# A fused adaLN attention block: the loads, the zero products and the first query evacuation of the prologue rearranged

## Chip, cores and metric

The kernel runs on one core of one Trainium2 chip. The metric is the device time of one launch in microseconds (us); a kernel is timed in several runs and the median counts. The profile is of one execution, whose span (first to last instruction of the core) is a little shorter than its device time.

## What is computed

The reference, cut to what matters (batch 1, 2048 tokens, width 512, 32 heads of 16, hidden width 1376):

```python
mod = (silu(c) @ w_mod).reshape(1, 6, 1, 512)       # sa, ca, ga, sb, cb, gb
h = layernorm(x) * (1 + ca) + sa
q, k, v = heads(h @ wqkv)
o = softmax(q @ k.T * 16 ** -0.5) @ v               # 32 heads, 2048 x 2048 scores each
x = x + ga * (o @ wo)
h = layernorm(x) * (1 + cb) + sb
x = x + gb * (gelu(h @ w1 + b1) @ w2 + b2)
```

## The kernel before, in words

Tokens lie in four blocks of 512 (`xb[0]` to `xb[3]`), channels in four chunks of 128. Four heads share a 128-row chunk in two parities, so a "quad" is (query block, chunk, parity): four heads, one in each 32-row strip of TensorE. One unit of work is one strip of one quad against one tile of 128 keys: a product of 32 rows into a PSUM bank (line 905), then the exponential, then the product with V (line 1144). The exponential is shared out: ScalarE takes two or three banks in one ACTIVATE (line 1382, tiles `PB` and, early, `TB`), VectorE takes others by writing a 16-bit integer that is read as a float (line 1526) and shifting it for its second and third copies (line 1560).

The program has two parts. The **prologue** (lines 141 to 393) is written out by hand: loads are issued, 12 zero products are put on TensorE (`turn_over(WARM[0])`, line 362), VectorE takes the statistics of `xb[0]` (line 212, four tiles), aggregates them (217), GpSimd makes the reciprocal root `rs` (222, 223), `silu_c` makes `sc_bf` from the condition vector `cc_bf` (an exponential on ScalarE, line 197, and three small VectorE operations, 198 to 200), TensorE makes the first shift and scale (32 products with one column, line 245, weights `W_m0`), three more zero products follow (`turn_over(WARM[1])`), VectorE normalises `xb[0]` (231), TensorE turns it (16 transposes, line 377), `hT` is evacuated by VectorE (274) and ScalarE (271) in turn, and chunk 0 of K and Q is projected (line 385, K and Q alternating over four pieces, weights `W_k` and `W_q`). `kT` is evacuated by ScalarE (285). The query has two masked halves: VectorE writes `qm[:, 0]` (388), ScalarE `qm[:, 1]` (389); the second is read only by quads of the second parity.

Loads go out on two queues, each in program order: SP's has half of `xb[0]`, half of `W_m0`, `W_k`, `W_q`, `W_v`, `xb[2]`, `xb[3]`, `W_m1`, later `W_m2` and `W_o`; ScalarE's has the other half of `xb[0]`, `cc_bf` (512 elements of two bytes, each to a place of its own), the other half of `W_m0` and `xb[1]`. Each large load is 512 KB (`W_m1`, `W_m2`: 1 MB).

The **body** is written by a planner that runs while the program is built. It keeps a clock for each engine (`clk`), assumed durations and due times, and emits one instruction after another; the order on each engine is then fixed, and the chip only waits on semaphores. `dve_load` adds up the VectorE work that is outstanding, and `d_wanted` offers further scores to VectorE only while that is below a limit, `D_LOAD` (1700 before). Where TensorE has nothing to do in the plan, `pe_idle` writes a zero product (line 1225 or 1228). `FRONT` holds the times at which the planner takes `W_v` and the blocks of `xb` for loaded. A **tail** ends the program: the last half block's output projection, second layernorm, MLP (lines 730 to 812) and stores.

Of the kernel before, what the change touches and what calls it, by code (L numbers as in the profile page):

```python
# [20 lines left out]
P = 128  # L21
# [30 lines left out]
D_BANKS = (5, 6, 2)  # L52
BG_BANKS = (2, 5, 6)
BG_STRICT = False
D_LOAD = 1700.0
X_FREE = 1
D_ALONE = 900.0
A_SLACK = 1350.0
OVER = 180.0
PART_MIN = 3  # L60
PV_FIRST = 99
D_SOON = 400.0
A_MIN = 600.0
D_WAIT = 350.0
POOL_WAIT = 4000.0
POOL_COVER = 1100.0
LOCK_WAIT = 100.0
TIE = 60.0
T_NEED = 1
T_NEXT = 1  # L70
T_OPEN = 0.0
ROOT = 1000.0
ROOT_L = 700.0
SPREAD = (0.9, 0.9, 0.65)
WARM = (12, 3)
FRONT = (1200.0, 0.0, 2600.0, 4000.0)
AHEAD = 32
T_KEEP = 3
# [22 lines left out]
def adaln_block(ctx: ExitStack, tc: tile.TileContext, A_x, A_wqkv, A_wo, B_x, B_w1, B_b1, B_w2, B_b2,  # L101
# [43 lines left out]
    for i, eng in enumerate((nc.sync, nc.scalar)):  # L145
        for t in (2 * i, 2 * i + 1):
            eng.dma_start(out=xb[0][:, t, :], in_=x_tok[0][:, t, :])
    nc.scalar.dma_start(out=cc_bf, in_=c.rearrange("o (j p) -> p (o j)", p=P))
    for i, eng in enumerate((nc.sync, nc.scalar)):
        eng.dma_start(out=W_m0[:, 2 * i:2 * i + 2, :], in_=wm_v[:, 2 * i:2 * i + 2, 0:2 * D])  # L150
    nc.sync.dma_start(out=W_k, in_=wqkv_v[:, :, D:2 * D])
    nc.scalar.dma_start(out=xb[1], in_=x_tok[1])
    nc.sync.dma_start(out=W_q, in_=wqkv_v[:, :, 0:D])
    nc.sync.dma_start(out=W_v, in_=wqkv_v[:, :, 2 * D:3 * D])
    for b in range(2, NQB):
        nc.sync.dma_start(out=xb[b], in_=x_tok[b])
    W_m1 = load_mod(1, nc.sync)


    AFTER = mybir.DependencyInfo(mybir.DependencyClass.Sync, mybir.DependencyReason.SCHED_ONLY)  # L160
# [203 lines left out]
    turn_over(WARM[0])  # L364
    st0 = pron.tile([P, 12, 6], FP32, name="st1")
    for t in range(4):
        ln_stats(xb[0], st0, t, t)
    psm = bk(7, FP32, 16)
    mv0, rs0 = ln_rstd(st0, 4)
    silu_c()  # L370
    first_mod_mm(psm)
    turn_over(WARM[1])
    turned = [bk(2 + j, BF16) for j in range(NC)]
    for t in range(4):
        ln_norm(xb[0], xb[0], mv0, rs0, t, t)
# [10 lines left out]
    k_evac(psk, 0, 0, "act")  # L386
    qm[(0, 0)] = qmp.tile([P, 2, 512], BF16, name="qm")
    nc.vector.tensor_scalar(out=qm[(0, 0)][:, 0, :], in0=psq, scalar1=qmask[:, 0:1], scalar2=None, op0=ALU.mult)
    nc.scalar.mul(out=qm[(0, 0)][:, 1, :], in_=psq, mul=qmask[:, 1:2])
    W_m2 = load_mod(2, nc.sync)  # L390
    nc.sync.dma_start(out=W_o, in_=A_wo.rearrange("(j p) n -> p j n", p=P))

# [109 lines left out]

    rdy[("k", 0, 0)], rdy[("q", 0, 0)] = 800.0, 1000.0
    rdy["wv"] = FRONT[0]
    for b in (1, 2, 3):
        rdy[("x", b)] = FRONT[b]
    for j in range(NC):
# [348 lines left out]
    def dve_cost(n):  # L856
        return 67.0 + 533.0 * n

    clk = {"PE": 0.0, "ACT": 1350.0, "DVE": 950.0, "POOL": 0.0}
    mode = [None]  # L860
    free = [0.0] * 6 + [850.0, 0.0]
    rowq = [[(qi, kt) for qi in range(QN) for kt in tiles_of(qi)] for _ in range(4)]
# [19 lines left out]
    outs = deque()  # L882
    stat = {"d": 0, "groups": 0, "part": 0, "bursts": 0}

    def item_ok(qi, kt, t):
        b, tq = quads[qi]
        ch = tq // 2
        return has([("k", ch, x // 4) for x in kt] + [("q", ch, b)], t)

    def tok_of(qi):  # L890
        if qi < LAST:
# [69 lines left out]
    def d_wanted(t):  # L961
        if len(d_fill) >= 2 or not any(rowq):
            return False
        if sum(len(q) for q in rowq) < 10:
            return False
        need = T_NEED if not units or len(units[-1]["it"]) == 2 else 0
        if need and min(q[0][0] for q in rowq if q) > cur[0]:
            need += T_NEXT
        if need and sum(1 for x in tslot if x <= t) < need + int(T_OPEN * len(units)):
            return False  # L970
        return dve_load(t) < D_LOAD

    def bg_bank(t):
        for i in ((6,) if X_BOTH else (5, 6)) if scored[0] < X_FRONT else BG_BANKS if any(rowq) else (2, 5, 6, 0, 1, 3, 4):
# [41 lines left out]
    def pe_burst(t, z):  # L1016
        bs = list(ZONES[z]) if z is not None else []
        x = EXTRA[z] if z is not None else None
        if scored[0] < X_FRONT:
            if z is not None:  # L1020
                x = 2 if z == 0 else 5 if X_BOTH else None
            if x is not None and free[x] <= t:
                bs.append(x)
        elif (x is not None and free[x] <= t and not (busy_sum[0] is None and reserve(t))
                and sum(1 for i in D_BANKS if free[i] <= t) > X_FREE):
            bs.append(x)
        take = []
        held_ = later_held()
        for r in lag_rows():
            if len(take) == len(bs):  # L1030
                break
            k = first_ok(r, t, held_ + len(take))
            if k is not None:
                take.append((r, k))
        if z is not None and len(take) < len(bs):
            more = [(r, k + 1) for r, k in take if len(rowq[r]) > k + 1 and item_ok(*rowq[r][k + 1], t)
                    and (rowq[r][k + 1][0] == rowq[r][k][0] or not k)]
            take += more[:len(bs) - len(take)]
        if z is not None and not take:
            return False  # L1040
        picked = [(r, rowq[r][k]) for r, k in take]
        for r, x in picked:
            rowq[r].remove(x)
        used = [r for r, _ in take]
        dp = []
        if d_wanted(t):
            for r in d_rows(used):
                k = next_d(r, t)
                if k is None:
                    continue  # L1050
                b_ = next((i for i in D_BANKS if free[i] <= t and i not in bs[:len(take)] + [x[0] for x in dp]), None)
                if b_ is None:
                    break
                if (not BG_STRICT and busy_sum[0] is None and reserve(t)
                        and sum(1 for i in BG_BANKS if free[i] <= t and i not in FLEX) - len(dp) < 2):
                    break
                dp.append((b_, r, rowq[r].pop(k)))
                if len(dp) + len(d_fill) >= 2 or z is not None and len(dp) + len(take) >= 4:
                    break
                u = units[-1] if units else None  # L1060
                if u is None or len(u["it"]) + len(dp) == 2:
                    break
        if z is None and not dp:
            return False
        go("q")
        t0 = clk["PE"]
        rows = [r for r, _ in picked] + [r for _, r, _ in dp]
        first = len(set(rows))
        clk["PE"] = t0 + group(first) + (group(len(rows) - first) if len(rows) > first else 0.0)
        ready = clk["PE"] + L_PE  # L1070
        qk([(b_, qi, kt, r) for (r, (qi, kt)), b_ in zip(picked, bs)] + [(b_, qi, kt, r) for b_, r, (qi, kt) in dp])
        for (r, (qi, kt)), b_ in zip(picked, bs):
            free[b_] = INF
        if z is not None:
            zone_busy[z] = True
            filled.append((z, [(qi, kt, r) for r, (qi, kt) in picked], clk["PE"] + L_PA))
        for b_, r, (qi, kt) in dp:
            free[b_] = INF
            if not units or len(units[-1]["it"]) == 2:
                s = next(i for i in range(NT) if tslot[i] <= t)  # L1080
                tslot[s] = INF
                units.append({"it": [], "a": {"s": s}, "j": 0, "n": 0})
            u = units[-1]
            u["it"].append((qi, kt, r))
            todo[qi][r] += NV - 1
            claimed[qi][r] += 1
            d_fill.append((b_, u, len(u["it"]) - 1, ready))
            stat["d"] += 1
        stat["bursts"] += 1
        return True  # L1090

    def pv_ready(t, press):
        qi = cur[0]
        if qi >= QN:
            return None
        if not od_open[0] and od_free[0] > t:
            return None
        g = []
        most = max(todo[qi])
        closed = not any(left[qi])  # L1100
        for r in range(4):
            e = entries[qi][r]
            if todo[qi][r] == 0:
                continue
            if e and e[0][0] <= t + 20 and has([("vv", x, e[0][3]) if e[0][3] else ("v", x) for x in e[0][2]], t):
                g.append(r)
            elif not (closed and todo[qi][r] < most) and not press:
                return None
        return g or None
# [132 lines left out]
    def step_pe_work(t):  # L1242
# [5 lines left out]
        tried = False  # L1248
        dw = d_wanted(t)
        d_at = min((free[i] for i in D_BANKS), default=INF)  # L1250
        later = dw and t < d_at < t + D_SOON and slack - (d_at - t) > A_MIN
        if fill_z is not None and slack < A_SLACK and not later:
            if pe_burst(t, fill_z):
                return True
            tried = True
        nxt = INF
        if any(rowq) and not tried:
            if fill_z is not None:
                nxt = max(t + max(0.0, slack - A_SLACK), d_at if later else 0.0)
            else:  # L1260
                cand = [max(free[i] for i in ZONES[z]) for z in (0, 1) if max(free[i] for i in ZONES[z]) < INF]
                if cand:
                    nxt = max(min(cand), t + slack - A_SLACK)

        if t > pe_at[0] + 700.0:
            nxt = INF

        def fits(x, m):
            return t + x + (0 if mode[0] == m else MODE) <= nxt + OVER
        if dw and dve_load(t) < D_ALONE and fits(226.0, "q") and nxt > t + D_WAIT:  # L1270
            if pe_burst(t, None):
                return True
        press = p_free() < 3 or sum(1 for x in tslot if x <= t) < 2
# [8 lines left out]
                return True  # L1282
        if not g:
            g = pv_ready(t, True)
            if g and len(g) < PART_MIN:
                g = None
        if g and fits(226.0, "p"):
            pe_pv(t, g)
# [459 lines left out]
```

## Time and profile before

| | us |
|---|---|
| median of 3 runs (757.05 to 758.9) | 757.85 |
| the profiled execution: device time | 755.97 |
| its span | 754.2 |
| TensorE busy in the span, zero products included | 736.8 |
| ScalarE busy | 721.3 |
| VectorE busy | 701.1 |
| GpSimd busy | 110.8 |
| first exponential of the body begins | 18.90 |

A row of the timeline is: start in us, duration in us, engine, line, operation, output <- input, form, count, and in brackets how long the engine sat idle before it and what ended that. Rows are merged where like instructions follow each other; SPq and ACTq are DMA issues on these queues. A row of the windows has a stretch, its length, and the busy time (and count) of each engine, then the granted TensorE clock, the DMA share and GB/s.

### The profile page before, as it was taken

The page shows a single profiled execution, that of the slowest core. Times are in us where ns is not written, and L with a number is a line of the kernel's source. Part 1 is how long each engine was busy: PE and PEld are TensorE (multiplying, and loading weights), DVE is VectorE, ACT ScalarE, POOL GpSimd, SP SyncE. Part 2 cuts the span into 40 slices and gives each one's busy share as a digit, 9 for nine tenths or more (in the row PEclk, how much of TensorE's full clock was granted, in tenths as well). Part 3 has the DMA queues.
Part 4 walks back from the last instruction along what each step waited for, and adds up shares of the span by engine and source line. Part 5 has one row for each costly group of instructions (what it writes and reads, how often), then busy time and mean ns, then how long its engine had stood idle before and what let it go on. Part 6 is the DMA issues. An engine that isn't in the chain of part 4 may idle for free. (4 is left out here: it accounts for less than half of the span.)

```text
span 754.2 us, 21382 instructions
## 1 busy us (share of the span) xinstructions
PE 736.8 (98%) x8858; PEld 257.9 (34%) x8861; DVE 701.1 (93%) x1444; ACT 721.3 (96%) x736; POOL 110.8 (15%) x136
## 2 busy tenths in 40 slices
PE   7999999999999999999999999999999999999997
PEld 3333332222333333224222232322233322444454
DVE  4976999999999999999999999999999999999983
ACT  2999999999999999999999999999999999999993
POOL 2424010311222310101001020100101110010000
PEclk8999999999999999999999999999999999999999
DMA  8200000001400100000001000000001010000000
GB/s 287 105 2 3 17 9 9 5 10 34 135 10 9 38 9 10 3 9 10 17 17 46 10 10 10 10 23 16 14 10 53 6 23 10 12 22 20 6 7 32
DMA packets 28456, 20.49 MB, mean 27 GB/s; under 512 B 14545, under 2 KB 24402, under 8 KB 28354
## 3 DMA queue, kind: packets, MB, share of 16 engines
q1 hardware_dynamic: 24914, 15.04, 7.6%
q10 hardware_dynamic: 3440, 4.03, 1.7%
q8 instruction: 71, 1.16, 0.7%
q14 instruction: 31, 0.25, 0.1%
HBM read 16.45 MB, written 2.61 MB: 25 GB/s over the span
## 5 line engine op out<-in xcount | busy, mean ns | idle before, releaser
L1382 ACT ACTIVATE PB<-PS 128x1024 bf16<-128x1024 f32 (+1 forms) x689 | 672.7, 1204 | 3.4 <-PE PS L905 2.0
L1526 DVE TENSOR_SCALAR TB<-PS 128x512 int16<-128x512 f32 (+1 forms) x527 | 367.2, 711 | 9.1 <-PE PS L905 7.6
L905 PE MATMUL PS<-qm,kT 32*128 32x512 bf16 (+1 forms) x2304 | 294.8, 358 | 3.2 <-ACT PB L1382 1.6
L1144 PE MATMUL PS<-PB,VE 128*32 128x512 bf16 (+1 forms) x1653 | 251.2, 361 | 0.0
L1560 DVE TENSOR_SCALAR TB<-TB 128x1024 int16<-128x1024 int16 x556 | 222.5, 424 | 4.6 <-PE PS L905 0.5
L1144 PE MATMUL PS<-TB,VV 128*32 128x512 f16 (+1 forms) x1246 | 217.9, 360 | 0.4 <-DVE TB L1560 0.2
L905 PEld LDWEIGHTS <-kT 32*128 32x128 bf16 x2304 | 82.7, 91 | 255.6 <-issue 251.6
L1144 PE MATMUL PS<-TB,VE 128*32 128x512 f16 (+2 forms) x651 | 148.4, 362 | 0.9 <-DVE o_sb L1475 0.5
L1144 PEld LDWEIGHTS <-VE 128*32 128x32 bf16 x2304 | 70.3, 94 | 78.3 <-issue 73.1
L1225 PE MATMUL PS<-W_q,zero 128*32 128x256 bf16 x471 | 94.0, 273 | 2.5 <-DVE TB L1526 1.8
L1144 PEld LDWEIGHTS <-VV 128*32 128x32 bf16 x1246 | 56.2, 95 | 40.2 <-issue 36.9
L1503 POOL TENSOR_TENSOR o_sb<-o_sb,rb 128x512 f32<-128x512 f32 (+1 forms) x16 | 19.3, 1204 | 253.4 <-DVE TB L1560 208.1
L1225 PEld LDWEIGHTS <-zero 128*32 128x32 bf16 x471 | 42.7, 96 | 33.1 <-issue 10.6
L1503 POOL TENSOR_TENSOR OT<-o_sb,rb 128x512 bf16<-128x512 f32 (+1 forms) x16 | 19.3, 1205 | 212.5 <-DVE TB L1560 154.3
L442 PE MATMUL PS<-h2T,W 128*32 128x512 bf16 x528 | 45.4, 383 | 0.0
L442 PE MATMUL PS<-W,uG 128*32 128x512 bf16 x528 | 45.4, 383 | 0.0
L645 DVE TENSOR_SCALAR uG<-PS,b1c 128x512 bf16<-128x512 f32 x33 | 24.6, 746 | 0.0
L442 PE MATMUL PS<-W_o,OT 128*32 128x512 bf16 x272 | 22.5, 383 | 0.0
L317 DVE CAST VE<-PS 128x512 bf16<-128x512 f32 x16 | 11.0, 687 | 11.4 <-PE PS L442 11.4
L1475 DVE COPY o_sb<-PS 128x512 f32<-128x512 f32 (+1 forms) x32 | 20.8, 649 | 0.7 <-PE PS L1144 0.7
L322 POOL TENSOR_SCALAR VV<-VE 128x512 bf16<-128x512 bf16 x12 | 18.0, 1504 | 21.5 <-DVE VE L317 21.0
L442 PE MATMUL PS<-hT,W_q 128*32 128x512 bf16 x240 | 21.0, 384 | 0.0
(122 smaller groups left out, 429.2 us busy)
## 6 DMA issues: line engine op xcount, KB each, us to landing
rb<-d SPq DMA_DIRECT2D x112, 32.0 KB
W_m<-in_w_mod_dram SPq DMA_DIRECT2D x2, 1024.0 KB
out_dram<-ob SPq DMA_DIRECT2D x16, 128.0 KB
xr<-in_A_x_dram SPq DMA_DIRECT2D x3, 512.0 KB
W<-in_B_w_dram ACTq DMA_DIRECT2D x1, 1376.0 KB
W<-in_B_w_dram ACTq DMA_DIRECT2D x1, 1280.0 KB
xb<-in_A_x_dram SPq DMA_DIRECT2D x2, 512.0 KB
W_m<-in_w_mod_dram SPq DMA_DIRECT2D x1, 512.0 KB
```

The lines of the kernel that those rows point to most:

```text
L317: nc.vector.tensor_copy(out=dst, in_=src)
L322: return nc.gpsimd.tensor_scalar(out=dst, in0=src, scalar1=WJ[j], scalar2=None, op0=ALU.mult)
L442: nc.tensor.matmul(out=ps[cols, :], lhsT=lhsT[:, cols], rhs=rhs, start=start, stop=stop)
L645: return lambda ps, e: nc.vector.tensor_scalar(out=T["u"][:, fc, :], in0=ps, scalar1=late["b1c"][:, fc:fc + 1], scalar2=None, op0=ALU.add)
L905: nc.tensor.matmul(out=bk(bank)[:, seg(qi, i)], lhsT=kT[32 * r:32 * r + 32, ch, kt[i] * P:(kt[i] + 1) * P], rhs=qm[(b, ch)][32 * r:32 * r ...
L1144: nc.tensor.matmul(out=PS[32 * r:32 * r + 32, 7, tok_of(qi)], lhsT=wt, rhs=src[:, seg(qi, i)], start=not started[qi][r], stop=todo[qi][r] ...
L1225: nc.tensor.matmul(out=PS[0:32, b_, 0:256], lhsT=zero, rhs=W_q[:, 0, 0:256], start=True, stop=True)
L1382: nc.scalar.activation(out=dst, in_=PS[:, b0:b0 + n, :], func=ACT.Exp, bias=-KEXP * math.log(2.0), scale=math.log(2.0) / STEP)
L1475: made = nc.vector.tensor_copy(out=o[:, cs], in_=PS[:, 7, cs])
L1503: return nc.gpsimd.tensor_tensor(out=(o if par else ot)[:, cs], in0=o[:, cs], in1=rb[:, cs], op=ALU.mult)
L1526: made = nc.vector.tensor_scalar(out=TB[:, u["a"]["s"], i:i + n, :], in0=PS[:, b0:b0 + n, :], scalar1=T_BIAS, scalar2=0.0, op0=ALU.add, op ...
L1560: made = nc.vector.tensor_scalar(out=TB[:, s, 0:n, :], in0=TB[:, a["s"], 0:n, :], scalar1=float(MJ[j] - MJ[j - 1]), scalar2=None, op0=ALU.add)
```

## The change

1. `cc_bf` is loaded from GpSimd's queue, ahead of everything else on it, in place of ScalarE's.
2. All loads after `xb[0]`, `cc_bf` and `W_m0` go on SP's queue, and the first of them, `W_k`, waits until the second of the four statistics of `xb[0]` is made. The order is then `W_k`, `W_q`, `xb[1]`, `W_v`, `xb[2]`, `xb[3]`, `W_m1`.
3. `WARM` goes from (12, 3) to (16, 3), and the call that used the 3 goes: 16 zero products before the first shift and scale, none between it and the transposes.
4. `qm[:, 1]` is no longer evacuated in the prologue but is a step of the planner on ScalarE, which may come behind the first exponentials; quads of the second parity wait for it (label `q01`), and the planner takes ScalarE for free at 650 in place of 1350.
5. The planner's constants become a table by stage whose rows are all alike. All values are those of before but `D_LOAD`, which goes from 1700 to 1900.

```diff
-D_LOAD = 1700.0
+TUNE = ((1900.0, 900.0, 1350.0, 180.0, 400.0, 600.0, 3, 1),) * 17
-WARM = (12, 3)
+WARM = (16, 3)
...
-    nc.scalar.dma_start(out=cc_bf, in_=c.rearrange("o (j p) -> p (o j)", p=P))
+    nc.gpsimd.dma_start(out=cc_bf, in_=c.rearrange("o (j p) -> p (o j)", p=P))
     for i, eng in enumerate((nc.sync, nc.scalar)):
         eng.dma_start(out=W_m0[:, 2 * i:2 * i + 2, :], in_=wm_v[:, 2 * i:2 * i + 2, 0:2 * D])
-    nc.sync.dma_start(out=W_k, in_=wqkv_v[:, :, D:2 * D])
-    nc.scalar.dma_start(out=xb[1], in_=x_tok[1])
-    nc.sync.dma_start(out=W_q, in_=wqkv_v[:, :, 0:D])
-    nc.sync.dma_start(out=W_v, in_=wqkv_v[:, :, 2 * D:3 * D])
-    for b in range(2, NQB):
-        nc.sync.dma_start(out=xb[b], in_=x_tok[b])
-    W_m1 = load_mod(1, nc.sync)
...
     turn_over(WARM[0])
     st0 = pron.tile([P, 12, 6], FP32, name="st1")
     for t in range(4):
-        ln_stats(xb[0], st0, t, t)
+        seen = nc.vector.bn_stats(out=st0[:, t, :], in_=xb[0][:, t, :])
+        if t == 1:
+            held = nc.sync.dma_start(out=W_k, in_=wqkv_v[:, :, D:2 * D])
+            tc.add_manual_dep(held.ins, seen.ins.name, AFTER, reason="order of loads")
+            nc.sync.dma_start(out=W_q, in_=wqkv_v[:, :, 0:D])
+            nc.sync.dma_start(out=xb[1], in_=x_tok[1])
+            nc.sync.dma_start(out=W_v, in_=wqkv_v[:, :, 2 * D:3 * D])
+            for b in range(2, NQB):
+                nc.sync.dma_start(out=xb[b], in_=x_tok[b])
+            W_m1 = load_mod(1, nc.sync)
...
-    turn_over(WARM[1])
...
-    nc.scalar.mul(out=qm[(0, 0)][:, 1, :], in_=psq, mul=qmask[:, 1:2])
...
+    op("ACT", 690.0, lambda: nc.scalar.mul(out=qm[(0, 0)][:, 1, :], in_=psq, mul=qmask[:, 1:2]), "q01", [], 5)
...
-    clk = {"PE": 0.0, "ACT": 1350.0, "DVE": 950.0, "POOL": 0.0}
+    clk = {"PE": 0.0, "ACT": 650.0, "DVE": 950.0, "POOL": 0.0}
...
+    def tv(i):
+        return TUNE[min(scored[0] >> 7, len(TUNE) - 1)][i]
...
-        return dve_load(t) < D_LOAD
+        return dve_load(t) < tv(0)
```

The instruction lists of the two programs differ in the body as well, since the planner starts from other clocks and another `D_LOAD`. Before and after: ScalarE exponentials of two banks (`PB`, `TB`) 598 + 14 and 590 + 12, of three banks 90 and 96; `hT` evacuations on ScalarE 2 and 3, on VectorE 14 and 13; VectorE exponentials of one bank 501 and 521, of two banks 26 and 17; shifts of two banks 550 and 554, of one 6 and 2; in the tail, hidden pieces evacuated by VectorE 8 and 9, by ScalarE 14 and 13; zero products of the planner 547 and 567.

More of the change, by code (lines that the diff above doesn't have):

```diff
@@ L54 @@
 BG_STRICT = False
-D_LOAD = 1700.0
[L56 to L60, printed above, removed]
 PV_FIRST = 99
-D_SOON = 400.0
-A_MIN = 600.0
 D_WAIT = 350.0
@@ L887, in item_ok @@
         ch = tq // 2
-        return has([("k", ch, x // 4) for x in kt] + [("q", ch, b)], t)
+        return has([("k", ch, x // 4) for x in kt] + [("q", ch, b)] + (["q01"] if qi == 1 else []), t)
     def tok_of(qi):
@@ L1024, in pe_burst @@
         elif (x is not None and free[x] <= t and not (busy_sum[0] is None and reserve(t))
-                and sum(1 for i in D_BANKS if free[i] <= t) > X_FREE):
+                and sum(1 for i in D_BANKS if free[i] <= t) > tv(7)):
             bs.append(x)
@@ L1095, in pv_ready @@
             return None
-        if not od_open[0] and od_free[0] > t:
+        if not od_open[0] and (od_free[0] > t or rdy.get("q01", INF) > t):
             return None
@@ L1250, in step_pe_work @@
         d_at = min((free[i] for i in D_BANKS), default=INF)
-        later = dw and t < d_at < t + D_SOON and slack - (d_at - t) > A_MIN
-        if fill_z is not None and slack < A_SLACK and not later:
+        later = dw and t < d_at < t + tv(4) and slack - (d_at - t) > tv(5)
+        if fill_z is not None and slack < tv(2) and not later:
             if pe_burst(t, fill_z):
@@ L1258, in step_pe_work @@
             if fill_z is not None:
-                nxt = max(t + max(0.0, slack - A_SLACK), d_at if later else 0.0)
+                nxt = max(t + max(0.0, slack - tv(2)), d_at if later else 0.0)
             else:
@@ L1262, in step_pe_work @@
                 if cand:
-                    nxt = max(min(cand), t + slack - A_SLACK)
+                    nxt = max(min(cand), t + slack - tv(2))
         if t > pe_at[0] + 700.0:
@@ L1268, in fits @@
         def fits(x, m):
-            return t + x + (0 if mode[0] == m else MODE) <= nxt + OVER
-        if dw and dve_load(t) < D_ALONE and fits(226.0, "q") and nxt > t + D_WAIT:
+            return t + x + (0 if mode[0] == m else MODE) <= nxt + tv(3)
+        if dw and dve_load(t) < tv(1) and fits(226.0, "q") and nxt > t + D_WAIT:
             if pe_burst(t, None):
@@ L1284, in step_pe_work @@
             g = pv_ready(t, True)
-            if g and len(g) < PART_MIN:
+            if g and len(g) < tv(6):
                 g = None
```

## Prediction

> **What bounds the kernel now.** I read the page's head first, then three stretches of the windows: prologue, body, tail.
>
> ```profile
> span 754.2 us, 21382 instructions
> ...
> core 0: us, PE busy (x) PEld busy (x) DVE busy (x) ACT busy (x) POOL busy (x), PEclk, DMA share, GB/s
> 0.00:18.90 18.90, 13.71 (x86) 6.54 (x87) 8.22 (x28) 4.15 (x6) 5.37 (x40) 0.82 0.87 287
> 18.90:729.20 710.30, 703.14 (x8604) 238.86 (x8601) 681.55 (x1393) 706.80 (x713) 104.49 (x94) 1.00 0.08 20
> 729.20:754.20 25.00, 19.96 (x177) 12.46 (x173) 11.35 (x25) 10.38 (x18) 0.94 (x2) 0.99 0.08 25
> ```
>
> In the body ScalarE (ACT) is busy 706.80 of 710.30 us: it is idle 3.5, VectorE (DVE) 28.75. TensorE's 703.14 contains the planner's zero products and is no bound. So the body is as long as ScalarE's work, and whatever lets the first exponential start sooner shortens the whole, as long as ScalarE stays fed. In the prologue no engine is full. There the order in time tells what ends last:
>
> ```profile
> 1.22 5.26 PE L362 MATMUL PS<-kT,zero 128*32 128x512 bf16 x12 [1.22 <-DVE kT L143]
> 1.65 0.46 ACTq L148 DMA_DIRECT2D cc_bf<-in_c_dram  x1
> 1.68 0.44 SPq L150 DMA_DIRECT2D W_m<-in_w_mod_dram  x1
> 3.67 2.52 DVE L212 BATCH_NORM_STATS2 st<-xb 128x6 f32<-128x512 bf16 x4 [1.50 <-DMA xb<-in_A_x_dram]
> 4.50 0.99 POOL L358 MEMSET rb<- 128x512 f32 x2
> 5.77 4.41 SPq L156 DMA_DIRECT2D xb<-in_A_x_dram  x2
> 6.11 0.36 DVE L217 BATCH_NORM_AGGREGATE mv<-st 128x2 f32<-128x6 f32 x4
> 6.57 0.23 POOL L222 TENSOR_SCALAR rs<-mv 128x4 f32<-128x4 f32 x1 [1.08 <-DVE mv L217]
> 6.88 1.04 POOL L223 TENSOR_TENSOR rs<-rs,half 128x4 f32<-128x4 f32 x1
> 7.94 0.21 ACT L197 ACTIVATE ce<-cc_bf 128x4 f32<-128x4 bf16 x1 [2.77 <-DMA cc_bf<-in_c_dram]
> 8.18 0.17 DVE L198 TENSOR_SCALAR ce<-ce 128x4 f32<-128x4 f32 x1 [1.70 <-ACT ce L197]
> 8.68 1.37 DVE L231 TENSOR_SCALAR xb<-xb,mv,rs 128x512 bf16<-128x512 bf16 x4
> 9.57 0.20 PE L245 MATMUL PS<-sc_bf,W_m 128*128 128x1 bf16 x2 [3.09 <-DMA W_m<-in_w_mod_dram]
> 10.12 0.96 PE L245 MATMUL PS<-sc_bf,W_m 128*128 128x1 bf16 x30 [0.35 <-DMA W_m<-in_w_mod_dram]
> 11.01 1.46 PE L362 MATMUL PS<-kT,zero 128*32 128x512 bf16 x3
> 12.40 1.89 PE L377 MATMUL PS<-ident,xb 128*128 128x128 bf16 x16
> 14.11 1.45 ACT L271 ACTIVATE hT<-PS,modc 128x512 bf16<-128x512 bf16 x2 [5.96 <-PE PS L377]
> 16.63 0.38 PE L385 MATMUL PS<-hT,W_q 128*128 128x512 bf16 x1
> 16.85 0.38 PE L385 MATMUL PS<-hT,W_k 128*128 128x512 bf16 x1
> 17.27 0.59 ACT L285 CAST kT<-PS 128x512 bf16<-128x512 f32 x1 [1.71 <-PE PS L385]
> 18.27 0.69 ACT L389 ACTIVATE qm<-PS,qmask 128x512 bf16<-128x512 f32 x1 [0.42 <-DVE qm L388]
> 18.46 0.39 PE L905 MATMUL PS<-qm,kT 32*128 32x512 bf16 x3
> 18.78 0.40 PE L442 MATMUL PS<-W_v,hT 128*32 128x512 bf16 x4
> 18.90 7.87 ACT L1382 ACTIVATE PB<-PS 128x1536 bf16<-128x1536 f32 x8
> ```
>
> TensorE waits for `W_m0` until 9.57 and 10.12, does the shift and scale until 11.08, three zero products, the transposes until 14.29, then the projection. The normalised `xb` was ready at 10.05, so the chain is: `W_m0`, then TensorE. The windows with only TensorE give the loads and the granted clock:
>
> ```profile
> core 0: us, PE busy (x), PEclk, DMA share, GB/s
> 2.00:4.00 2.00, 2.00 (x6) 1.00 0.85 256
> 4.00:5.00 1.00, 1.00 (x3) 1.00 0.22 64
> 5.00:9.50 4.50, 1.48 (x4) 1.00 0.95 330
> 9.50:16.50 7.00, 6.05 (x55) 0.52 1.09 349
> 16.50:18.90 2.40, 2.40 (x20) 0.99 1.06 374
> ```
>
> `xb[0]` (0.52 MB) moves from 2 to 4 us, then there is a hole of one us; from 5.0 to 9.5 1.49 MB move, of which `W_m0` is 1.05. And from 9.5 to 16.5 TensorE has half its clock, after an idle stretch from 6.5 to 9.6.
>
> **The change part by part.** *Loads held, `W_m0` alone.* 1.05 MB at 330 GB/s take 3.2 us: landed at 8.2 if the hole stays. The hole follows the issue of `cc_bf` (1.65, 512 pieces of two bytes) right before that of `W_m` (1.68); if that issue makes the hole, it goes with the move, and 7.2 is the earliest. The other end is 10.1, as before. I take 8.2, which leaves one us for landing if the hole goes. The hold itself costs nothing: the second statistic ends at about 3.67 + 2.52/2 = 4.9, and `W_k` has 3.3 us of `W_m0` ahead of it. Queued behind the waiting SP issue are all later loads. `W_q`, the second of them, ends at 2.1 MB: 1.49 by 9.5, the other 0.61 at 349 GB/s by 11.2 (10.2 without the hole). `xb[1]` follows at 12.8, `W_v` at 14.3.
>
> *`cc_bf` on GpSimd's queue.* No row shows a DMA issued there. Its nearest row is ScalarE's issue of the same load, 0.46 us; the dearest issues of the prologue are SP's two of 4.41 together, 2.2 each; below zero is excluded, since it is added to GpSimd. GpSimd's cover is the 1.08 us that it waits before `rs`. I take under 1.08, cost nothing; at 2.2, `rs` and all behind it are 1.1 late. Issue to use was 6.3 us (1.65 to 7.94); starting at 0.7 it is there by 7.0 at the latest. Then the three small VectorE operations (0.5 us) end at 7.1 to 7.7 and no longer stand between `rs` (7.92) and the normalisation, which goes from 8.05 to 9.4 in place of 8.68 to 10.05.
> The Trainium skill, SBUF — State Buffer, section "SBUF: two separate sides", speaks against this move: GpSimd writes such descriptors itself and is locked out while VectorE runs certain operations. VectorE has only about half a us of small clears then, so by that rule the sum would lose at most that, within the cover; no run here shows it.
>
> *Zero products.* Sixteen at 5.26/12 = 0.44 end at 8.2 at the latest, when `W_m0` lands: no cost. The three that go lay on the path: 1.46 less. The idle stretch shrinks from 3.1 us to under one. I take it that the clock stays full from then on; if not, each projection product costs 0.44 in place of 0.22.
> The Trainium skill, TensorE: Matmul & The Clock Gate, Part 1, says the clock is judged in free-running windows of about 3.4 us: full after a busy one, half after an idle one. The trace agrees: half after 3.1 us of idleness, full again 7 us later, two such windows. By it sixteen products always contain one whole window and twelve (5.3 us) need not.
>
> *The sum of the prologue.* Shift and scale 8.2 to 9.3 (1.1, as 0.20 + 0.96), beside the normalisation (9.4). The last four transposes follow, at most a quarter of 1.89: 9.9. The last `hT` ended 15.56, 1.27 behind the transposes' end of 14.29: now 11.2. `W_q` 11.2 as well. From the first Q product to the last K product there are five pitches of 0.22 (16.63 to 16.85): 12.3. From there to the first exponential it was 18.90 - 16.85 = 2.05: **14.35 in place of 18.90, 4.55 us sooner**. Ends: last K product right behind the last `hT`, 11.4, gains 5.45; half clock (five pitches of 0.44) and a landing one us later, 14.4, gains 2.45.
>
> *What is late next.* `W_v` (14.3) is wanted 1.93 behind the last K product, as 18.78 was: 14.2. The first exponential covers three banks and over a us, so a wait up to 15 costs nothing. `xb[1]` (12.8) is wanted once VectorE has written its query half, after 13.
>
> *Second query half.* It lay in a gap of ScalarE (17.86 to 18.90) and now lies in the full body: +0.69, and the first exponential gains under 0.1.
>
> *The new plan.* The two instruction lists differ by counts; these rows give the prices:
>
> ```profile
> 699.09 30.11 ACT L1382 ACTIVATE PB<-PS 128x1024 bf16<-128x1024 f32 x32
> ...
> 739.87 4.84 ACT L785 ACTIVATE uG<-PS,b1c 128x256 bf16<-128x256 f32 x11 [0.72 <-PE PS L776]
> ...
> L1526 DVE TENSOR_SCALAR TB<-PS 128x512 int16<-128x512 f32 x501 | 335.7, 685 | 9.0 <-PE PS L905 7.6
> L1526 DVE TENSOR_SCALAR TB<-PS 128x1024 int16<-128x1024 f32 x26 | 31.6, 1216 | 0.1
> L1560 DVE TENSOR_SCALAR TB<-TB 128x1024 int16<-128x1024 int16 x550 | 221.1, 425 | 4.5 <-PE PS L905 0.5
> ```
>
> ScalarE: ten two-bank exponentials fewer at 30.11/32 = 0.94, six of three banks more at 7.87 - 7 x 0.94 = 1.3: -1.6; one `hT` more, +0.72; one tail piece fewer, -0.44; with the query half **-0.6**, which I count as 0, since the pitches are of two spots. VectorE: 20 x 0.685 - 9 x 1.216 + 4 x 0.425 and an `hT` against a tail piece, about **+4.5**. Its 28.75 us of idleness cover that; if they don't, up to 4.5 come on top. Twenty more zero products of the planner fill TensorE's gaps: 0.
>
> Sum: 754.2 - 4.55 = 749.65 of span; with 755.97 - 754.2 = 1.77 around it 751.4. The profiled execution lay 1.88 below the median, so against that: **753.3 us**.
>
> **The rivals.** A run of this kernel can tell about 0.2%, 1.5 us, from no change.
>
> *The body starves (the other side).* `D_LOAD` 1900 lets TensorE score into VectorE's banks while VectorE still has more to do. TensorE and VectorE are in order; a bank that comes free late holds up the product for ScalarE behind it. Price: ScalarE's idleness in the body, 3.5 us now. It decides from 3.5 + 4.55 + 1.5 = 9.5 us on, 1.3% of the body; 6.5 to 9.5 us give no measurable change (756.3 to 759.3), and 12 us give 757.85 - 4.55 + 8.5 = 761.8. For it: VectorE is 96% busy and gets 4.5 us more. Against: two columns more in 555 change little, and ScalarE's idleness is small throughout.
>
> *The clock falls back, or `W_q` lands late.* Gain 2.45: 755.4. For it: the shift and scale is 32 tiny products and the waits for `hT` remain. Against: idleness under one us in one piece. (The skill's page on the clock gate counts busy windows; whether such a window passes, no run shows.)
>
> *GpSimd is held up by its DMA.* Above 1.08 us every further us delays `rs` and the normalisation; `W_q` at 11.2 hides little of it. At 4 us of issue, 3 late: 756.3.
>
> *`W_m0` gains nothing* (another limit than sharing): shift and scale at 10.1 as before; transposes at full clock 11.1 to 12.1, `hT` 13.4, exponential 15.7: 754.7, inside the forecast's range.
>
> *The new plan happens to run better*, ScalarE's idleness and mix -2: below 752.
>
> **How the numbers follow.** Forecast with `W_m0` case (752.0 to 755.0) 0.55; clock or late `W_q` (755 to 756) 0.12; GpSimd (755.5 to 757.5) 0.06; starved body 0.18, of which 0.11 over 759.4 and 0.07 within; better plan (750 to 752) 0.09. Faster: 0.55 + 0.12 + 0.02 + 0.09 = 0.78, of which I keep 0.76, as the clock's case touches the bound; same 0.13; slower 0.11. The range from 750.5 to 758.0 leaves out under 0.2: the worse half of the starved body and some of the better plan.
>
> **What would show it.** First exponential near 14.4; `W_m` waits ending near 8.2; no DMA hole from 4 to 5; GpSimd's `rs` still at 6.6 to 7.9; granted clock 1.0 in the transposes; no wait on `W_v` over half a us; ScalarE idle 3 to 5 us in the body. Wrong if the body from first to last exponential is over 2 us longer than 710.3, or if the first exponential comes after 16.5.

## The result, and the profile after

The changed kernel takes 759.82 us (median of 10 runs, 758.46 to 762.32); the kernel before took 757.21 beside it (10 runs). The ratio is 1.0037, 95% interval 1.0022 to 1.0052: **slower by 0.4%**, where 753.3 was forecast. The profiled execution took 759.09 us, its span 757.2.

The windows of the kernel after, cut where the prediction cut them (up to the first exponential, up to the last, the tail):

```profile
core 0: us, PE busy (x) PEld busy (x) DVE busy (x) ACT busy (x) POOL busy (x), PEclk, DMA share, GB/s
0.00:19.10 19.10, 12.95 (x87) 6.60 (x88) 8.43 (x28) 3.52 (x5) 6.35 (x41) 0.82 0.88 282
19.10:733.30 714.20, 705.45 (x8645) 242.11 (x8643) 681.26 (x1404) 707.04 (x711) 103.36 (x94) 1.00 0.07 20
733.30:757.20 23.90, 19.04 (x159) 10.69 (x158) 11.30 (x24) 10.01 (x17) 0.93 (x2) 0.96 0.08 25
```

ScalarE's work in the body is as forecast: 707.04 us against 706.80. Its idleness doubled, 7.2 us in place of 3.5, and the first exponential came no sooner (19.1 against 18.9). The tail is 1.1 us shorter. The forecast span was 749.65; of the 7.6 us between it and 757.2 the prologue makes 4.75 (19.1 in place of 14.35) and the body 3.9 (714.2 in place of 710.3), less the tail's 1.1. So there are two questions: why the prologue gained nothing in this execution, and where ScalarE's 3.7 us of new idleness lie. The order in time of the prologue after:

```profile
1.21 5.12 PE L348 MATMUL PS<-kT,zero 128*32 128x512 bf16 x16 [1.21 <-DVE kT L136]
1.24 0.99 POOL L141 DMA_DIRECT2D cc_bf<-in_c_dram  x1 [0.81 <-POOLq L1728]
4.97 0.37 SPq L355 DMA_DIRECT2D W_k<-in_A_wqkv_dram  x1
6.98 0.23 POOL L208 TENSOR_SCALAR rs<-mv 128x4 f32<-128x4 f32 x1
8.64 0.20 ACT L183 ACTIVATE ce<-cc_bf 128x4 f32<-128x4 bf16 x1 [5.23 <-DMA cc_bf<-in_c_dram]
9.38 1.38 DVE L217 TENSOR_SCALAR xb<-xb,mv,rs 128x512 bf16<-128x512 bf16 x4
10.74 0.99 PE L231 MATMUL PS<-sc_bf,W_m 128*128 128x1 bf16 x32 [4.41 <-DMA W_m<-in_w_mod_dram]
11.59 1.87 PE L371 MATMUL PS<-ident,xb 128*128 128x128 bf16 x16
16.29 0.63 PE L379 MATMUL PS<-hT,W_k 128*128 128x512 bf16 x1
18.68 0.39 PE L902 MATMUL PS<-qm,kT 32*128 32x512 bf16 x3
19.12 1.45 ACT L1379 ACTIVATE PB<-PS 128x1536 bf16<-128x1536 f32 x1 [1.58 <-PE PS L902]
20.46 0.68 ACT L498 ACTIVATE qm<-PS,qmask 128x512 bf16<-128x512 f32 x1
```

The condition vector arrived at 8.6, later than before (7.9); `W_m0` held TensorE until 10.74, also later; and the sixteen zero products were over at 6.33, since the clock rose under them (5.12 us for sixteen, where twelve had taken 5.26). TensorE then stood for 4.41 us. The windows with only TensorE give what that did:

```profile
core 0: us, PE busy (x), PEclk, DMA share, GB/s
2.00:4.00 2.00, 2.00 (x6) 1.00 0.92 279
4.00:5.00 1.00, 1.00 (x5) 1.00 0.66 166
5.00:9.50 4.50, 1.33 (x7) 1.00 0.84 268
9.50:16.50 7.00, 5.22 (x54) 0.62 1.10 354
16.50:18.90 2.40, 2.40 (x14) 0.70 1.07 371
```

The clock was at half again, now into the 18th us, so the first score product came 2.4 us behind the last K product, where it had taken 1.6. The hole at 4 to 5 us filled up (166 in place of 64 GB/s), but 5.0 to 9.5 moved less than before (268 against 330). Nor was `W_m0` alone: the hold ended at 4.97, when `W_k` went out. SP's queue moved 1.17 MB up to 9.5, and its halves of `xb[0]` and `W_m0` are only 0.79 of that; so 0.4 MB of `W_k` had moved, and 0.8 MB of later loads by 10.7, while the last packets of ScalarE's half of `W_m0` moved only between 9.5 and 10.7. Before, the other loads had moved 0.7 MB when `W_m0` released TensorE at 10.1.

ScalarE's new idleness lies in one stretch, at two spots. These rows of the kernel after are from 187 to 201 us:

```profile
187.33 0.43 ACTq L561 DMA_DIRECT2D W<-in_B_w_dram  x1
187.81 2.02 ACTq L565 DMA_DIRECT2D W<-in_B_w_dram  x1
187.94 2.12 SPq L571 DMA_DIRECT2D b_bf<-in_B_b_dram  x1
187.96 0.68 DVE L1472 COPY o_sb<-PS 128x512 f32<-128x512 f32 x1
...
189.88 9.15 ACT L1379 ACTIVATE PB<-PS 128x1536 bf16<-128x1536 f32 x8 [1.38 <-PE PS L1141]
...
190.58 0.52 SPq L1477 DMA_DIRECT2D d<-o_sb  x1
...
197.08 0.36 SPq L1479 DMA_DIRECT2D dall<-d  x1
...
198.83 0.25 DVE L1491 RECIPROCAL rp<-dall 128x16 f32<-128x16 f32 x1 [2.48 <-DMA dall<-d]
...
199.42 0.38 PE L1141 MATMUL PS<-TB,VV 128*32 128x512 f16 x1 [1.61 <-DVE TB L1557]
...
200.78 2.37 ACT L1379 ACTIVATE PB<-PS 128x1536 bf16<-128x1536 f32 x2 [1.75 <-PE PS L902]
```

At the end of every quad its four rows of denominators go out to DRAM (`d`, 8 KB), come back spread over the partitions (`dall`), and VectorE takes their reciprocal (`rp`). Here the MLP's weights (2.7 MB) were issued at 187.3, just ahead of that. `d` took 6.5 us to land, the whole round trip 10.2 (188.64 to 198.83), VectorE stood before `rp` for 2.48 us, TensorE behind VectorE for 1.61, ScalarE behind TensorE for 1.75. The other spot is the 1.38 us before 189.88. The profile names TensorE there, but the gap ends 0.05 us behind ScalarE's own issue of the second large load, which took 2.02 us (187.81 to 189.83) where it had taken 0.52. In the kernel before, the same stretch is:

```profile
183.92 0.50 SPq L1480 DMA_DIRECT2D d<-o_sb  x1
185.38 0.38 ACTq L567 DMA_DIRECT2D W<-in_B_w_dram  x1
185.61 0.34 SPq L1482 DMA_DIRECT2D dall<-d  x1
185.80 0.52 ACTq L571 DMA_DIRECT2D W<-in_B_w_dram  x1
...
190.01 0.25 DVE L1494 RECIPROCAL rp<-dall 128x16 f32<-128x16 f32 x1 [0.18 <-DMA dall<-d]
```

`d` was out 1.5 us ahead of the weights and landed in 1.7 us; only the way back met them (4.4 us from the issue of `dall` to `rp`). The round trip took 6.1 us and VectorE waited 0.18. The planner takes the weights and the denominators for independent and puts `rp` where some 6 us are over: in the runs below in which it does not wait it begins 5.9 to 6.6 us behind `o_sb` as well.

### The profile page after: what moved, and what is told of

Its sections match the earlier page's. It is cut to its first block, busy times and chain, and to the rows that moved or that the text cites. A ratio compares the mean times of both kernels' runs of the same rounds, so it can differ in the third digit from the quotient of the medians.

```text
span 757.2 us, 21449 instructions
## 1 busy us (share of the span) xinstructions
PE 737.4 (97%) x8885; PEld 259.4 (34%) x8888; DVE 701.0 (93%) x1455; ACT 720.6 (95%) x732; POOL 110.6 (15%) x137
## 3 DMA queue, kind: packets, MB, share of 16 engines
q10 hardware_dynamic: 2384, 3.51, 1.5%
## 4 chain that ended last, share of the span: by engine, by line
PE 64%; ACT 22%; DVE 5%; issue 5%; DMA 2%; SPq 0%; DVEq 0%; ACTq 0%
PE PS L902 22%; PE PS L1141 21%; ACT PB L1379 21%; PE PS L435 14%; PE PS L1222 3%; DVE TB L1523 3%; DVE TB L1557 2%; PE PS L770 2%; PE PS L799 1%; DMA W_m<-in_w_mod_dram 1%; DMA d<-o_sb 1%; ACT uG L649 1%; PE PS L1225 1%; PE PS L222 1%; ACT L1379 0%
## 5 line engine op out<-in xcount | busy, mean ns | idle before, releaser
L1141 PE MATMUL PS<-PB,VE 128*32 128x512 bf16 (+1 forms) x1654 | 254.0, 361 | 0.0
L1141 PE MATMUL PS<-TB,VV 128*32 128x512 f16 (+1 forms) x1252 | 221.3, 360 | 1.8 <-DVE TB L1557 1.8
L1557 DVE TENSOR_SCALAR TB<-TB 128x1024 int16<-128x1024 int16 x556 | 219.9, 419 | 3.3
L1141 PEld LDWEIGHTS <-VE 128*32 128x32 bf16 x2304 | 72.4, 94 | 81.3 <-issue 75.3
L1222 PE MATMUL PS<-W_q,zero 128*32 128x256 bf16 x497 | 96.2, 274 | 1.3 <-DVE TB L1523 0.9
L1222 PEld LDWEIGHTS <-zero 128*32 128x32 bf16 x497 | 46.0, 96 | 33.7 <-issue 11.1
L435 PE MATMUL PS<-h2T,W 128*32 128x512 bf16 x528 | 47.3, 383 | 0.0
L1503 POOL TENSOR_TENSOR OT<-OT,o_sb 128x512 bf16<-128x512 bf16 (+1 forms) x16 | 17.6, 1100 | 32.3 <-DVE TB L1557 30.1
L435 PE MATMUL PS<-hT,W_k 128*32 128x512 bf16 x240 | 20.9, 385 | 0.0
```

Source lines behind the costliest of these rows:

```text
L435: nc.tensor.matmul(out=ps[cols, :], lhsT=lhsT[:, cols], rhs=rhs, start=start, stop=stop)
L1141: nc.tensor.matmul(out=PS[32 * r:32 * r + 32, 7, tok_of(qi)], lhsT=wt, rhs=src[:, seg(qi, i)], start=not started[qi][r], stop=todo[qi][r] ...
L1222: nc.tensor.matmul(out=PS[0:32, b_, 0:256], lhsT=zero, rhs=W_q[:, 0, 0:256], start=True, stop=True)
L1503: return nc.gpsimd.tensor_tensor(out=ot[:, cs], in0=ot[:, cs], in1=o[:, cs], op=ALU.add)
L1557: made = nc.vector.tensor_scalar(out=TB[:, s, 0:n, :], in0=TB[:, a["s"], 0:n, :], scalar1=float(MJ[j] - MJ[j - 1]), scalar2=None, op0=ALU.add)
```

## Experiments

Each was timed in rounds with the kernel before on the same chip; a ratio is to that, with its 95% interval.

**Prologue or body.** The edits separate cleanly: the first two kernels have exactly the old body's order behind the new prologue, and the new body's order behind the old one (TensorE's products in the body number 8604 before and in pro_only, 8645 in plan_only and in the changed kernel).

```diff
# pro_only, on the changed kernel: second query half back in the prologue, and
-TUNE = ((1900.0, ...
+TUNE = ((1700.0, ...
-    clk = {"PE": 0.0, "ACT": 650.0, ...
+    clk = {"PE": 0.0, "ACT": 1350.0, ...
# plan_only, on the changed kernel: loads, cc_bf and WARM = (12, 3) as before
# dload_only, on the kernel before
-D_LOAD = 1700.0
+D_LOAD = 1900.0
# q01_only: plan_only with 1700
```

> The changed prologue (condition vector on GpSimd's queue, held loads, zero products 16 and 0) before the old body: D_LOAD 1700, second query half in the prologue, ScalarE free at 1350, so every instruction of the body stands in the order of before. Theory P (the loss is the planner's new order): the prologue is about neutral, first exponential within 0.3 us of 18.9, ScalarE idle 3 to 5 us in the body, time within 0.8 us of before. Rival L (the loss comes from the prologue, whose later loads and late clock starve the body): 2 to 3 us slower than before.

> The prologue of before (loads, condition vector, 12 and 3 zero products) with the changed body: D_LOAD 1900, second query half as a planned step, ScalarE free at 650. Theory P: 2 to 3 us slower than before, ScalarE idle 7 to 9 us in the body. Rival L: within 0.8 us of before.

> The kernel of before with D_LOAD 1900 alone. If the limit itself harms (VectorE's queue longer, banks late): slower by 1 to 3 us with ScalarE's idleness up by as much. If only the order as such changes, with no direction of its own: anywhere from 2 us faster to 3 us slower, and not the sum's partner of q01_only.

> The kernel of before with the second query half as a planned step behind the first exponential and ScalarE free at 650, D_LOAD 1700. By the ledger of ScalarE: +0.7 us, since the half lay in a gap before. If a new order as such costs: 1 to 3 us slower with idle stretches of ScalarE at places far from the prologue.

Measured: pro_only 754.21 us, ratio 0.9967 (0.9955 to 0.998); plan_only 762.85, 1.0077 (1.0058 to 1.0095); dload_only 764.13, 1.0102 (1.0086 to 1.0117); q01_only 763.33, 1.0096 (1.0078 to 1.0115). The prologue is a gain of 2.5 us, better than theory P expected; the body's new order costs 6.1. Of the 1.9 us between the two profiled spans 1.1 lie in the prologue (first exponential at 17.78 in place of 18.90). Each of the two planner edits alone costs 7, so they do not add up. In all three slow ones VectorE waits longer at the round trip than in the changed kernel (4.38, 5.01 and 2.74 us), and ScalarE's issue of the second large load is short (0.5 to 0.6 us). In plan_only and dload_only ScalarE's longest wait is behind that (4.09 and 4.71 us). In q01_only it is not: behind the round trip ScalarE waits 1.21 and 1.04, and 3.51 us at 374.6, where TensorE is full and no DMA is waited for. So the round trip explains only a part of q01_only, and no run has it with later loads. About 1 us of dload_only's 7.4 lies outside of the core's span, where it spends 2.8 us and the other kernels 1.8; why is not known. In dload_only:

```profile
198.32 0.25 DVE L1494 RECIPROCAL rp<-dall 128x16 f32<-128x16 f32 x1 [5.01 <-DMA dall<-d]
...
199.17 0.80 PE L1225 MATMUL PS<-W_q,zero 128*32 128x256 bf16 x3 [4.58 <-DVE TB L1526]
```

and its windows there, on all engines:

```profile
185.00:195.00 10.00, 9.59 (x109) 2.97 (x108) 8.27 (x16) 9.90 (x11) 1.01 (x4) 1.00 0.96 272
195.00:200.00 5.00, 0.83 (x7) 0.35 (x6) 1.68 (x4) 0.85 (x1) 1.69 (x2) 0.66 0.16 29
200.00:205.00 5.00, 5.00 (x33) 0.82 (x32) 3.88 (x8) 3.03 (x3) 0.00 (x0) 0.50 0.13 30
205.00:210.00 5.00, 5.00 (x50) 1.56 (x47) 4.37 (x9) 4.37 (x6) 0.81 (x1) 0.82 0.01 2
```

TensorE's 4.58 us of waiting are enough to halve its clock up to about 207 us, and ScalarE is busy 8.25 of these last 15 us: a wait of VectorE of 5.0 us costs ScalarE 6.8. In the changed kernel TensorE waited 1.61 us there and the clock stayed full; in after_ccact below it waited 2.05 and the clock was at 0.50 from 202.5 to 207.5.

**What limits the prologue.** Four kernels from the changed one, all with its body, so their times contain the stall; what they tell is read from the rows of the prologue.

```diff
# after_pj: four neighbouring rows to a partition, for the vector and for w_mod
-c.rearrange("o (j p) -> p (o j)", p=P)          w_mod.rearrange("(j p) n -> p j n", p=P)
+c.rearrange("o (p j) -> p (o j)", p=P)          w_mod.rearrange("(p j) n -> p j n", p=P)
# after_warm30
-WARM = (16, 3)
+WARM = (30, 3)
# after_ccact
-    nc.gpsimd.dma_start(out=cc_bf, ...
+    nc.scalar.dma_start(out=cc_bf, ...
# after_nohold: the loads behind W_m0 issued at once, as before
```

> The changed kernel with the condition vector and w_mod both laid out so that each partition holds four neighbouring rows: the vector then moves in 128 pieces of 8 bytes in place of 512 of 2 bytes, on the same queue. Theory S (the small pieces hold up the DMA engines: the vector itself and W_m0 behind them): ce begins under 7.5 in place of 8.64, the shift and scale starts at 8 to 9.5 in place of 10.74, no hole in the loads at 7 to 8 us. Rival G (GpSimd's queue as such is slow to land): ce still after 8.3, W_m0 no sooner.

> The changed kernel with 30 zero products ahead of the shift and scale in place of 16. Theory C (sixteen ended at 6.3, four us of idleness halved the clock): zero products last to about 9.3, granted clock 1.0 in transposes and projection, transposes about 1.1 us in place of 1.87, first exponential 2 to 3 us sooner (16.3 to 17.2), time 1.5 to 3 us less than the changed kernel. Rival: the clock falls anyway during the 32 tiny products and the waits for hT, first exponential within 0.5 us of 19.1.

> The changed kernel with the condition vector back on ScalarE's queue, ahead of its half of W_m0. Theory S: it lands at about 8 as before (7.94), W_m0 lands by 9.5 to 10 since the later loads are held. If GpSimd's queue helps W_m0: W_m0 later than 10.7.

> The changed kernel with the later loads issued at once, in the order and on the queues of before. If the hold helps W_m0: shift and scale starts over 0.5 us later than 10.74. If W_m0 is limited by something else than sharing: within 0.5 us of 10.74, and the loads move over 250 GB/s at 7 to 8 us, where the hold leaves a hole.

Measured: after_pj 759.47 us, ratio 1.0036 (1.0022 to 1.0051); after_warm30 759.84, 1.0042 (1.0025 to 1.0059); after_ccact 761.28, 1.0053 (1.0035 to 1.0072); after_nohold 763.2, 1.0072 (1.0044 to 1.01).

With pieces of 8 bytes `ce` began at 5.47 in place of 8.64, and the normalisation then waited for `rs` (8.17): theory S holds for the vector in this execution. But `W_m0` released TensorE at 9.75, no better than in pro_only, whose prologue is that of the changed kernel (9.83): for `W_m0` it fails. On ScalarE's queue the vector came at 8.97 and `W_m0` at 10.30; the queue makes little difference. Without the hold `ce` came at 9.42, `W_q` made TensorE wait another 1.13 us and the first exponential began at 20.29, and the ratio is above the changed kernel's (1.0072 for 1.0037); yet the hole at 7 to 8 us was there as well (107 GB/s, 126 in the changed kernel), so the hold does not make it. It is not in every execution: pro_only moved 325 GB/s there. Over all profiled executions, those of the kernels below too, the six with the old prologue released TensorE from `W_m0` at 9.2 to 11.4 (mean 10.6), the five with the new prologue unaltered at 9.0 to 10.7 (mean 10.0): at `W_m0` the changed prologue is worth some 0.6 us, less than one execution differs from the next, not the two that were forecast. What slows `W_m0` between 5 and 9 us is not settled; a hold that lasts until `W_m0` has landed was not tried.

With 30 zero products theory C holds. The rows of after_warm30:

```profile
1.21 7.93 PE L348 MATMUL PS<-kT,zero 128*32 128x512 bf16 x30 [1.21 <-DVE kT L136]
...
9.58 0.95 PE L231 MATMUL PS<-sc_bf,W_m 128*128 128x1 bf16 x32 [0.44 <-DMA W_m<-in_w_mod_dram]
10.39 1.05 PE L371 MATMUL PS<-ident,xb 128*128 128x128 bf16 x16
...
15.62 1.45 ACT L1379 ACTIVATE PB<-PS 128x1536 bf16<-128x1536 f32 x1 [1.05 <-PE PS L902]
...
196.19 0.25 DVE L1491 RECIPROCAL rp<-dall 128x16 f32<-128x16 f32 x1 [4.68 <-DMA dall<-d]
```

The first exponential came 3.5 us sooner, and the time did not move: the wait at the round trip was 4.68 us in that execution, the clock halved there too, and the body took 717.7 us in place of 714.2. The stall took back what the prologue had gained.

**The stall taken away.** The loads of the MLP's weights and biases are issued 12 exponentials later. TensorE, VectorE and GpSimd keep their instruction orders word for word; on ScalarE's queue only the two large loads move, on SP's the small ones go behind the denominators' four steps.

```diff
# after_latew; open_late() collects the loads, and exp_to() issues them
+    for f in (big, little): later.append(f)      # W_1, W_2 / last rows of W_2, b1, b2
+    count_down[0] = 12
...
+        if later:
+            count_down[0] -= 1
+            if count_down[0] == 0:
+                for f in later: f()
+                later.clear()
# after_latebig: only big() later.  dload_latew: dload_only with both later.
# warm30_latew: after_latew with WARM = (30, 3)
```

> The changed kernel with the loads of the MLP's weights and biases (both large ones on ScalarE's queue, the small ones on SP's) issued 12 exponentials later; the orders of TensorE, VectorE and GpSimd stay word for word. Theory R (the new order puts a quad's denominator round trip, 188 to 199 us, behind these loads; VectorE's reciprocal waits 2.5 to 5 us, TensorE idles, the clock may halve): that wait falls under 0.5 us, ScalarE's idleness in the body falls from about 9 to 4 to 6 us, time 3 to 5 us less than the changed kernel, 755 to 757. Rival O (the new order costs by many small waits everywhere): under 1 us less.

> The same with only the two large loads (2.7 MB) issued later, the small ones where they were, ahead of the round trip on SP's queue. If the 2.7 MB in the DMA engines make the round trip late: as good as with both later. If the small ones on the same queue do (two-byte pieces, 2.1 us of issue): the wait stays over 1.5 us.

> The kernel of before with D_LOAD 1900 alone (7.4 us slower than before, a wait of 5.0 us of the reciprocal and 10 us at half clock), with the same loads issued 12 exponentials later. Theory R: the wait and the half clock go, 5 to 7 us less, within 2.5 us of before. Rival O: still 5 us or more slower than before.

> The changed kernel with 30 zero products and the later weight loads together. The 30 zero products brought the first exponential 3.5 us forward (15.62) and no time, with a wait of 4.68 us at the round trip. Theory R: with that wait gone the 3.5 us come through: 752 to 754, faster than before by 3 to 5 us. Rival O: no better than the later loads alone.

Measured: after_latew 754.56 us, ratio 0.9966 (0.9955 to 0.9976); after_latebig 755.11, 0.9972 (0.9962 to 0.9982); dload_latew 758.28, 1.0018 (1.0005 to 1.0032); warm30_latew 753.49, 0.9954 (0.994 to 0.9967). Theory R holds: the same instructions in the same order, but for the time of a few loads, take the changed kernel from 0.4% slower to 0.3% faster, and dload_only from 1.0% slower to 0.2%; that 0.2% is the 1 us outside of its span. Of the 3.5 us that 30 zero products gave the first exponential, 1.1 come through (754.56 to 753.49). In after_latew:

```profile
186.07 0.68 DVE L1491 COPY o_sb<-PS 128x512 f32<-128x512 f32 x1
186.78 0.50 SPq L1496 DMA_DIRECT2D d<-o_sb  x1
188.47 0.34 SPq L1498 DMA_DIRECT2D dall<-d  x1
192.89 0.24 DVE L1510 RECIPROCAL rp<-dall 128x16 f32<-128x16 f32 x1
...
198.55 0.39 ACTq L571 DMA_DIRECT2D W<-in_B_w_dram  x1
```

`d` lands in 1.7 us, `rp` begins 6.1 us behind `o_sb` without a wait, ScalarE's issues take 0.39 and 0.53 us, and its body is 710.9 us long with ScalarE busy 706.95 of them, as before the change:

```profile
17.20:728.10 710.90, 704.89 (x8645) 241.59 (x8646) 681.42 (x1404) 706.95 (x711) 103.42 (x94) 1.00 0.08 21
```

With only the large loads moved the small ones stood ahead of `d` on SP's queue still, which went out 1.5 us behind the end of `o_sb` (187.84) and landed in 1.7. In after_latebig:

```profile
189.30 0.51 SPq L1496 DMA_DIRECT2D d<-o_sb  x1
...
191.00 0.36 SPq L1498 DMA_DIRECT2D dall<-d  x1
```

The gain was the same within the intervals: the 2.7 MB under way in the DMA engines are what makes 8 KB late, though they are on another queue. Moving them also takes away the 1.38 us at ScalarE's issue, so in the changed kernel itself the two are told apart by the trace alone; plan_only and dload_only have the round trip without the long issue.
The Trainium skill, DMA: Bandwidth & Descriptors, section "Issuing engines are not separate DMA queues", says that transfers from all issuing engines run on the same 16 DMA engines and interleave. The runs agree: 6.5 us for `d` on SP's queue with the weights on ScalarE's, 1.7 us without.

**Controls, and the best.**

```diff
# plan_latew: plan_only with both loads later.  pro_latew: pro_only with both loads later.
# best_pj: warm30_latew with the layout of after_pj
```

> The prologue of before with the changed body (6.1 us slower than before) and the weight loads 12 exponentials later. If the round trip behind these loads is all that the new order costs: within 1.5 us of before. If the order costs more by itself (ScalarE's query half, a gap of 1.3 us of ScalarE at 63 us): 2 to 3 us slower still.

> A control: the changed prologue with the old body (2.5 us faster than before), where the round trip is over when the weight loads go out, and the same later loads. Theory R: no gain, within 0.8 us of the changed prologue with the old body. If later weight loads help any order (less load on the DMA engines, ScalarE's issue): 2 us or more faster than that.

> The changed kernel with 30 zero products, the condition vector in pieces of 8 bytes (w_mod laid out to match) and the later weight loads. If the prologue's gains add up: 752 to 753.5, the fastest of all; if the normalisation, not the vector, sets the prologue with 30 zero products: equal to 30 zero products with later loads, 753.5.

Measured: plan_latew 756.29 us, ratio 0.9994 (0.9982 to 1.0005); pro_latew 755.87, 0.9981 (0.9971 to 0.9991); best_pj 753.72, 0.9951 (0.9934 to 0.9968). The new body behind the old prologue, 0.8% slower with the stall, is level with before without it: the collision with these loads is the whole cost of the new order, within the interval. Later loads do not help the old order, in which `d` had landed first (0.9981 against 0.9967, worse by 1.1 us where 0.8 was expected at most, though the intervals overlap). best_pj and warm30_latew are equal and the fastest, 0.5% under the kernel before; in best_pj `ce` began at 7.46, so the 5.47 of after_pj is not dependable, and `W_m0` (10.35) sets its prologue.

## Why the prediction was wrong, point by point

- **The step that failed: "The new plan".** I priced the new order by the counts of its instructions and set it to 0. The counts were right: ScalarE's work in the body changed by 0.2 us. What changed was where a small round trip stands relative to two large loads. It cost ScalarE over 3 us in the profiled execution (1.38 and 1.75) and 6.1 us of time in plan_only, more than the prologue gained. VectorE's +4.5 us did not come either (681.26 in the body for 681.55), mainly because 554 shifts took 0.419 us each where 550 had taken 0.425.
- **The rival "the body starves"** named the side and the quantity to watch, ScalarE's idleness, but a wrong mechanism. It was not scores waiting for VectorE's banks under a higher `D_LOAD`: dload_latew keeps the higher limit and is level but for the 1 us outside of its span. The place was in the profile of before: the weights go out at 185.38, 1.5 us behind `d`, and `rp` already waits 0.18 us. A margin that thin was the thing to find; a shift of 2.8 us consumed it (`o_sb` ended 1.5 us ahead of the weights before and 1.3 us behind them after).
- **Prologue, sign right, size off.** 4.55 us forecast, 2.5 measured (pro_only), and none in the profiled execution. Two terms were mis-sized. `W_m0` released TensorE at 9.0 to 10.7, not 8.2: "Loads held, `W_m0` alone" put all of `W_m0` ahead of `W_k`, but half of it goes out on ScalarE's queue, and SP's went on to `W_k` meanwhile; nor did the rate of 330 GB/s hold (268). And "I take it that the clock stays full" failed: transposes 1.87 us as before, K and Q products 0.43 apart. I took the old pitch of 0.44 for all sixteen zero products; the clock rose under them, they ended two us sooner than I had them, and the idle stretch was longer than before (4.41 against 3.09 us). In the four other executions with this prologue unaltered the sixteen took 5.8 to 6.4 us, 1.95 to 3.17 us of idleness followed, and the transposes took 1.87 there too.
 The Trainium skill, TensorE: Matmul & The Clock Gate, Part 1, that I cited, puts the half clock behind an idle window of about 3.4 us. The runs differ: 1.95 us of idleness brought it in after_latew, as 3.09 had before the change, and 1.31 us in warm30_latew did not. "The trace agrees" was too much said; the measured 3.09 was the figure to go by.
- **The signs of being wrong** that the prediction named both came: the body was 3.9 us longer (2 was the limit), and the first exponential began at 19.1 (16.5 was the limit).
- **`cc_bf` on GpSimd's queue.** The issue took 0.99 us, inside the cover of 1.08 as taken, and `rs` began 0.41 us later than before. But "there by 7.0 at the latest" failed: 8.64. The queue is not the reason (5.9 to 7.6 us from issue to use on ScalarE's in seven executions, 6.3 to 8.2 on GpSimd's in eight); the 512 pieces may be, but one of the two executions with 128 pieces took 6.2 us as well. The lockout by VectorE, for which the prediction cites the Trainium skill, SBUF — State Buffer, section "SBUF: two separate sides", has no sign here: the same issue took 0.78 us in pieces of 8 bytes, on the same engine and at the same time.
- **Second query half**: 0.68 us in the body, as priced. **`W_v` and `xb[1]`**: no wait, as forecast. **The three zero products** left the path, as forecast.

## What to carry to other kernels

When a generated order changes, equal work says little: look for the instructions that wait for a DMA round trip in a strict order, read their margins in the old trace (here 0.18 us at `rp`, 1.5 us between `d` and the weights), and treat a margin below the expected shift as a price with its own chance. Before a gain at the start of a program is believed, ask which later wait could take it back; 3.5 us in the prologue were worth nothing here until two loads were moved, and 1.1 us then. A load is alone only until the next one goes out, on whichever queue (`W_k` here, at 4.97). And cover made of filler has to be sized by time at the clock that it will itself bring about.

## What the runs showed of the hardware that was not expected

- An 8 KB store took 6.5 us to land while 2.7 MB were under way on another queue (5.0 to 7.6 in the eight runs with that order), and 1.7 us otherwise.
- ScalarE's issue of a 1.3 MB load took 0.5 us in most executions and 2.0 us in three (the changed kernel, after_ccact, after_nohold); there ScalarE's next exponential began 1.35 to 1.39 us late. What makes the issue long is open.
- 512 pieces of two bytes took 6 to 8 us from issue to use on either queue, while 128 pieces of 8 bytes took 4.2 us in one execution and 6.2 in another.
- A wait of TensorE of 4.58 us in a full body halved its clock for most of 10 us, one of 2.05 us (after_ccact) did too, one of 1.61 us did not. At the start, 1.95 us did and 1.31 did not.
- `W_m0`, 1 MB, released TensorE between 9.0 and 11.4 us after the start, whichever prologue it was; the hole in the traffic at 7 to 8 us that some executions have is not explained. The gap of 1.29 us on ScalarE near 63 us in the kernels with the planned query half, which ends on no releaser in the profile, is open as well; it cost too little to be chased.
